# A fifth unit takes half of its gated features by eleven half products, in a new order of all steps

## The chip, the cores and the metric

The kernel runs on one core of one Trainium2 chip. The metric is the device time of one execution in microseconds (us), as the median over runs; lower is better. All arithmetic is fp32.

## The reference

Two blocks follow each other. The first is delta-rule attention over batch 4, 8 heads, 768 positions, head size 48; the second is a multiplicative feed-forward on the 3072 x 384 tokens that the first puts out.

```python
k_n = k / (norm(k) + 1e-06)
for t in range(S):                               # S = 768
    y[:, :, t] = q[:, :, t] @ state
    v_old = k_n[:, :, t] @ state
    state += beta_t * outer(k_n[:, :, t], v[:, :, t] - v_old)
x = y as (3072, 384)
a = x @ w1                                       # 384 -> 1024
b = x @ w2                                       # 384 -> 1024
out = ((a * b) @ w3) @ w_out                     # 1024 -> 1024 -> 384
```

## The kernel before

The engines are named as in the profile: PE multiplies matrices, DVE and POOL do elementwise work, ACT copies, SP starts transfers. The 768 positions go in 12 chunks of 64, for all 32 pairs of batch and head at once. Two chunks make a unit: 512 tokens. Units are numbered u = 0 to 5, and `last` is 5.

Each chunk m passes through the attention: its scores (`s`, lines 451 and 457), U and PT from them on DVE (463, 474), a triangular inverse per pair of chunks (`V`, the function `inverse`: 31 steps of two DVE instructions, lines 524 and 529, on a layout that goes out to DRAM and comes back, `Ud`, `Ub`), the corner blocks (`e`, 602 and 619), the chain that carries the state (`c`, line 672; 706, 717 and 738 on DVE) and the outputs (`y`, 777), which end as x transposed in `xT`.

Each unit then passes through the feed-forward. `w3 @ w_out` is folded into one matrix `w34` at the start (913), where all weights come in as fp64 and are converted piece by piece (`P0` to `P35`, 838 to 853). Units 0 to 4 compute a and b directly with `ab(u, jc)`: for a block of 128 features, three matmuls on `w1s` (934), a copy by ACT (946), three on `w2s`, and a multiplication on DVE (950). Unit 5 uses `features(u, p)`: for a pair p of blocks it splits tokens in two halves of 256 and forms a and b together by eleven half products of 128x256 (1074) where direct products would need twelve; sums of weights (`W`, `features_sums`, 1026 to 1037, on POOL) and of tokens (`X5`, `token_sums`, 1052, on POOL) feed it, DVE adds the pieces (1083), ACT copies them (1088 to 1110), and DVE multiplies (1118, 1131). Then `o(u)` computes the output by seven half products (1166), with sums of the a*b slabs (`S`, `slab_sums`, 1007: on POOL for units 0 to 4, on DVE for unit 5), and `result(u)` combines and stores (`x`, 1197 and 1182).

Products of the feed-forward go to four banks called `f` in turn (`ps_f`), the attention's to two double banks called `w` (`ps_w`). `in_turn` hands out buffers in a ring and skips those in `held`.

The order of all work is written out by hand. The string `ORDER` has one word for each step; each word names a part (`a42`: unit 4's `ab`, block 2; `V5`: the inverse of unit 5), and each time the word comes up, the part, a generator, goes on to its next `yield`:

```python
    for name in ORDER.split():
        step(name)
    in_text_order()
```

`in_text_order` ties the instructions of each engine together in that order, so the string sets the order on every engine.

Of the kernel before, what the change touches and what calls it, by code (L numbers as in the profile page):

```python
# [39 lines left out]
k0 g0 g0 g0 K0 V0 g0 k1 P12 K0 K0 beta K1 P0 g0 g0 K1 K1 g0 q1 P12 g0 P12 P12 beta g0 g0 beta N0  # L40
P8 P9 P8 P8 P8 P3 P0 P3 P3 P9 P0 s1 s1 s1 P9 s0 P3 P0 P13 P13 P13 s0 s0 V0 V0 V0 P1 P1 Q1 P1 P9
Q1 P10 P13 V0 V0 Q1 P1 P10 P2 P2 t0 t0 P2 P4 P4 V0 t1 P2 t1 V0 P4 P4 h1 t4 t4 N0 P6 f0 P7 P10
P10 P5 t2 t5 P18 V0 V0 P11 P6 V0 P6 P6 N0 P16 P19 V0 P7 P7 P5 P5 P5 q0 V0 t5 h1 P18 f2 P11 V0
P18 P7 t2 V0 f0 P14 h1 P22 P18 P19 f0 V0 P11 V0 V0 P11 P19 V0 V0 V0 P16 P16 P17 f2 f2 t10 t10
P23 Q0 Q0 t3 P19 t11 V0 P16 Q0 V0 t3 P22 P22 P22 P14 V0 V0 V0 f1 V0 V0 P23 P21 t8 P15 f1 P14 t11
P17 P17 f5 f5 V0 V0 f1 V0 V0 P17 t8 P15 V0 h0 V0 V0 P14 f5 P26 t6 P23 P20 V0 q2 P27 k2 t6 t9 t14
t9 v0 V0 P23 f4 f4 t14 f4 t15 t15 P21 P15 P15 t7 q3 V0 v1 Q2 Q2 V0 e0 h0 h0 e0 Q2 g1 e0 g1 t7 g1
f3 e0 e0 K2 P27 K2 e1 e0 e0 n0 e1 k3 f7 P27 n0 e1 c0 e1 P21 e1 f7 V1 g1 c0 y0 P28 c0 P20 P25 f7
P20 P20 P29 f3 P33 y0 n1 n1 P21 g1 c0 c1 y0 g1 g1 K2 f3 P28 P28 P28 P34 c1 t13 t13 t12 t12 P25
P27 K3 K3 K3 e1 s2 g1 P25 P29 P35 g1 P25 P33 f6 f6 P29 P29 e1 g1 N1 Q3 Q3 c1 y0 s2 s2 s2 P34 c1  # L50
s2 s2 f6 Q3 s3 K2 P30 P34 P34 P26 P26 P24 y1 y1 s3 P30 P31 N1 P33 N1 s3 b6 b6 P33 P35 P35 u2 P35
s3 s3 s3 Q0 P30 P30 c1 b4 b4 P24 P24 u3 P24 y1 b5 b5 b5 V1 P26 y1 V1 b5 P31 V1 P32 b6 b6 P31 b4
b0 b0 c1 b3 b4 b3 b7 V1 V1 b7 V1 V1 a02 V1 a02 V1 a03 V1 a05 V1 k4 V1 a00 V1 V1 P32 P32 a03 V1
b1 a00 a05 V1 V1 V1 V1 a04 V1 b1 c2 P32 P31 a04 a04 a04 a01 a01 T T T v2 n2 a02 T V1 k5 a07 a07
V1 v3 a02 V1 V1 a03 a03 V1 V1 V1 V1 V1 V1 a06 a06 b2 V1 b2 a07 a07 V1 a01 V1 V1 V1 a01 p4 p4 b2
n3 V1 V1 b2 a00 a00 a05 a05 g2 g2 g2 g2 a06 n2 b1 b1 b0 e2 b0 a06 g2 b3 b3 b7 b7 o0 g2 c2 n3 x0
e2 e2 g2 g2 o0 d4 e2 g2 e2 g2 o0 S0 S0 S0 e2 c2 d4 S0 S0 e3 S0 S0 x0 S0 S0 S0 S0 e3 e3 S0 S0 d4
p5 c2 c2 e3 c2 x0 S0 o0 c3 S0 e3 c3 o0 e3 N2 y2 c3 x0 o0 d4 p5 y2 S0 c3 y3 x0 x0 x0 d5 d5 s4 s4
o0 x0 y3 s4 s4 d5 d5 s4 s4 N2 s5 y3 u4 s5 V2 s5 s5 s5 N2 s5 c3 u5 V2 x0 p6 x0 a14 p6 a14 a14 a14
a13 a13 V2 V2 V2 V2 V2 a12 a12 V2 a16 a16 V2 V2 V2 V2 V2 V2 V2 a15 V2 a15 a11 a11 V2 V2 V2 V2 V2  # L60
V2 V2 V2 V2 v5 x0 V2 a10 V2 V2 k6 V2 v4 V2 V2 V2 V2 a17 a17 a15 a15 a10 k7 d6 d6 d6 a10 a10 c3
S1 n5 n4 a13 a12 a12 a13 V2 e4 a17 e4 a11 g3 g3 g3 g3 a11 Q3 c4 g3 g3 n4 c4 e4 a16 a16 e5 e4 e4
e4 o1 x1 S1 a17 S1 S1 S1 e5 e5 S1 e5 d6 n5 g3 c4 c4 g3 o1 S1 c4 V3 c4 g3 e5 e5 o1 p7 g3 N3 c5 p7
# [28 lines left out]
def kernel(  # L92
# [48 lines left out]
    turns, held = {}, set()  # L141

# [354 lines left out]
    def inverse(j):  # L497
# [15 lines left out]
        if j < 2:  # L513

            V = two_banks().rearrange("p a (s t) -> p (a s) t", t=BS)
            held.add(("w", turns["w"]))
# [14 lines left out]
        if j == 0:  # L531
            for x in range(4):
                dve.transpose(
                    out=TTpair[quarter(x), :, :, :, quarter(x % 2)].rearrange(
                        "s m r h t -> s t m (r h)"
                    ),
                    in_=V[quarter(x)].rearrange("p s t -> p t s"),
                )
                if x == 3:
                    held.clear()  # L540
                yield
            return
        if j < 2:
# [3 lines left out]
            held.clear()  # L547
# [417 lines left out]
    def weight_sums():  # L965
# [14 lines left out]
        Ts["T3"] = kperm[:].rearrange("p b a x d -> p (b a x d)")  # L980
# [12 lines left out]
    def slab_sums(u):  # L993
        for out_, x, y, op in (
# [4 lines left out]
        ):  # L999
            for i in range(HF if u < LU else HF // 2):  # L1000
                if u < LU:
                    o_, x_, y_ = (
# [356 lines left out]
```

## Time and profile before

| | before |
|---|---|
| median of 3 runs | 558.1 us (556.59 to 558.62) |
| profiled execution | 557.83 us, span 556.1 us |
| busy: PE, DVE, POOL, ACT | 533.6, 343.7, 169.7, 145.7 us |
| granted clock of PE | 1.00 |

The profile shows one execution. Busy times are shares of the span from the first to the last instruction; the execution's own time is 1.7 us longer than that span. Line numbers are those of the kernel before unless a passage speaks of the changed one, where most lines lie 7 to 30 further down (934 is 941, 950 is 957, 1074 is 1104, 1083 is 1113, 1166 is 1196, 1197 is 1227).

### The profile page before, as it was taken

What the parts mean: (1) busy time and instruction counts of PE and PEld (TensorE: products, weight loads), DVE (VectorE), ACT (ScalarE), POOL (GpSimd) and SP (SyncE); (2) the same over time, 40 slices, a digit from 0 to 9 for tenths busy, and PEclk for the clock granted to TensorE, in tenths of its full rate; (3) what the DMA queues carried; (4) which work ended last, traced back from release to release, by engine and by line L of the source; (5) the groups of instructions that cost most, each with busy time, mean ns of one, the idle gap of its engine ahead of it and who ended that gap; (6) DMA issues with size and microseconds to landing.
All of it is one profiled execution on the core that took longest, in us unless ns stands there. A gap on an engine that the chain in (4) does not pass through costs nothing.

```text
span 556.1 us, 19932 instructions
## 1 busy us (share of the span) xinstructions
PE 533.6 (96%) x8732; PEld 390.8 (70%) x8732; DVE 343.7 (62%) x800; ACT 145.7 (26%) x291; POOL 169.7 (31%) x213
## 2 busy tenths in 40 slices
PE   6699999999999999999999999999999999989997
PEld 5556667788998544888444897445995447988897
DVE  6799738589546498574995354885373973213552
ACT  2786567531121120220111211202201102212200
POOL 7574443527730002812102522004540027420000
PEclk9999999999999999999999999999999999999999
DMA  9999956594423593453745453605307222020001
GB/s 189 339 307 230 158 140 150 128 160 55 96 48 55 119 147 72 67 88 89 122 74 100 70 91 80 126 38 83 51 15 154 26 60 38 18 58 1 0 2 57
DMA packets 191527, 54.22 MB, mean 98 GB/s; under 512 B 178928, under 2 KB 185072, under 8 KB 191440
## 3 DMA queue, kind: packets, MB, share of 16 engines
q1 hardware_dynamic: 189328, 52.56, 46.3%
q8 instruction: 68, 1.11, 0.9%
q10 hardware_dynamic: 2112, 0.39, 0.5%
q14 instruction: 19, 0.16, 0.1%
HBM read 41.78 MB, written 9.96 MB: 93 GB/s over the span
## 4 chain that ended last, share of the span: by engine, by line
PE 93%; DVE 3%; issue 2%; DMA 2%; ACT 0%; SPq 0%; DVEq 0%
PE ps_f L934 38%; PE ps_f L1166 20%; PE ps_f L913 7%; PE ps_w L672 6%; PE ps_w L777 4%; PE ps_f L1074 4%; PE ps_w L619 3%; PE ps_w L1074 2%; PE ps_w L451 2%; PE ps_f L369 1%; PE ps_w L457 1%; PE ps_f L904 1%; DMA beta_fm<-in_beta_dram 1%; PE ps_w L409 1%; PE ps_w L1166 1%
## 5 line engine op out<-in xcount | busy, mean ns | idle before, releaser
L934 PE MATMUL ps_f<-xT,w2s 128*128 128x512 f32 (+1 forms) x288 | 106.9, 524 | 0.0
L934 PE MATMUL ps_f<-xT,w1s 128*128 128x512 f32 (+1 forms) x288 | 106.7, 524 | 0.0
L934 PEld LDWEIGHTS ps_f<-xT,w2s 128*128 128x128 f32 x288 | 54.1, 190 | 46.5 <-issue 41.6
L934 PEld LDWEIGHTS ps_f<-xT,w1s 128*128 128x128 f32 x288 | 54.0, 190 | 45.3 <-issue 41.6
L1007 POOL TENSOR_TENSOR ab<-ab 128x256 f32<-128x256 f32 x80 | 56.4, 731 | 78.7 <-DVE ab L950 73.8
L946 ACT COPY ab<-ps_f 128x512 f32<-128x512 f32 (+1 forms) x48 | 24.3, 515 | 134.4 <-PE ps_f L934 130.3
L1166 PE MATMUL ps_f<-w,ab 128*128 128x192 f32 x320 | 57.3, 332 | 1.9 <-DVE osb L1197 1.3
L1166 PEld LDWEIGHTS ps_f<-w,ab 128*128 128x128 f32 x320 | 51.6, 190 | 3.3 <-issue 2.4
L524 DVE TENSOR_TENSOR tb<-Vb,Ub 128x31 f32<-128x31 f32 (+15 forms) x124 | 43.0, 347 | 15.4 <-DMA Ub<-Ud 11.5
L529 DVE TENSOR_TENSOR Vb<-Vb,tb 128x31 f32<-128x31 f32 (+15 forms) x124 | 43.0, 346 | 4.3
L913 PE MATMUL ps_f<-wo,w3T 128*128 128x384 f32 x128 | 43.5, 491 | 0.4 <-ACT w3T L907 0.4
L1166 PE MATMUL ps_f<-room,ab 128*128 128x192 f32 x240 | 42.8, 332 | 0.0
L950 DVE TENSOR_TENSOR ab<-ab,ps_f 128x512 f32<-128x512 f32 (+1 forms) x48 | 27.4, 589 | 24.0 <-PE ps_f L934 24.0
L1166 PEld LDWEIGHTS ps_f<-room,ab 128*128 128x128 f32 x240 | 38.7, 190 | 0.7
L913 PEld LDWEIGHTS ps_f<-wo,w3T 128*128 128x128 f32 x128 | 23.5, 190 | 15.4 <-ACT w3T L907 0.5
L301 POOL TENSOR_TENSOR sq<-ktok 128x384 f32<-128x384 f32 x24 | 19.7, 835 | 43.5 <-DMA out_dram<-osb 16.9
L658 POOL TENSOR_TENSOR vtok<-vtok,n 128x384 f32<-128x384 f32 x24 | 19.8, 832 | 39.5 <-DMA vtok<-in_v_dram 39.5
L635 ACT COPY T<-ps_w 32x512 f32<-32x512 f32 x24 | 13.8, 577 | 67.2 <-PE ps_w L619 46.2
L795 ACT COPY xT<-ps_w 112x256 f32<-112x256 f32 x48 | 14.3, 384 | 65.0 <-PE ps_w L777 61.7
L451 PE MATMUL ps_w<-KQ 48*64 48x128 f32 x320 | 21.9, 274 | 1.8 <-DVE PT L474 1.5
L717 DVE TENSOR_TENSOR X<-ps_w,wt 128x768 f32<-128x768 f32 x12 | 11.5, 956 | 19.4 <-PE ps_w L672 12.9
L1197 DVE TENSOR_TENSOR room<-room,ps_f 128x384 f32<-128x384 f32 (+1 forms) x13 | 7.0, 537 | 26.4 <-PE ps_f L1166 26.4
(170 smaller groups left out, 805.9 us busy)
## 6 DMA issues: line engine op xcount, KB each, us to landing
vtok<-in_v_dram SPq DMA_DIRECT2D x24, 192.0 KB, 4.4
out_dram<-osb SPq DMA_DIRECT2D x23, 192.0 KB, 2.6
ktok<-in_k_dram SPq DMA_DIRECT2D x44, 96.0 KB, 3.4
raw<-in_moe_w_dram SPq DMA_DIRECT2D x8, 512.0 KB, 6.2
raw<-in_moe_w_dram SPq DMA_DIRECT2D x18, 192.0 KB, 4.5
raw<-in_moe_w_out_dram SPq DMA_DIRECT2D x7, 384.0 KB, 5.3
Ud<-U SPq DMA_DIRECT2D x40, 64.0 KB, 2.8
Ub<-Ud SPq DMA_DIRECT2D x5, 512.0 KB, 4.2
```

The costliest lines, as they stand in the source:

```text
L451: pe.matmul(ps[half(z), 0, n : n + 128], lhsT=x[:, 0, :], rhs=x.rearrange("p j t -> p (j t)"), start=True, stop=True,)
L524: dve.tensor_tensor(out=tv, in0=V[:, 0 : s + 1, s : s + 1].to_broadcast([P, s + 1, n]), in1=U[:, s, s + 1 : BS].unsqueeze(1).to_broadcast( ...
L529: dve.tensor_tensor(out=o, in0=o, in1=tv, op=ALU.subtract)
L672: pe.matmul(out(ps, r, h, z), lhsT=lhs(r, h, z), rhs=rhs(r, h, z), start=True, stop=True,)
L777: i = pe.matmul(region(h, z, r), lhsT=lhs, rhs=rhs, start=part[n] not in part[:n], stop=part[n] not in part[n + 1 :],)
L913: pe.matmul(ps[:, 0:DM], lhsT=w3Ts[jc, kc // 4][:, kc % 4 * P : kc % 4 * P + P], rhs=wo(kc), start=(kc == 0), stop=(kc == KF - 1),)
L934: pe.matmul(ps[:].rearrange("p b c t -> p b (c t)"), lhsT=w[:, m, js], rhs=x[:, m, :, c0:c1].rearrange("p b c t -> p b (c t)"), start=(m = ...
L946: act.copy(out=t, in_=ps)
L950: dve.tensor_tensor(out=t, in0=t, in1=ps, op=ALU.mult)
L1007: (dve if u == last else pool).tensor_tensor(out=o_, in0=x_, in1=y_, op=op)
L1074: pe.matmul(ps[:, j, :], lhsT=w[j], rhs=x, start=first and j == 0, stop=j == 1, skip_group_check=not first,)
L1166: pe.matmul(ps[b][:, b, :], lhsT=ab_of(u, HF * f + i, t0), rhs=ws_[w][:, i], start=first and i == 0 and (b == 0 or n == "F"), stop=i == HF ...
```

## The change

Four things change. `LU`, the first unit that uses half products, goes from 5 to 4: unit 4 takes blocks 0, 1, 4 and 5 directly (`a40` to `a43`) and the pairs p = 1 and p = 3 by `features` (`a44`, `a45`). The multiplications of pair 1 of unit 4 run on POOL, those of pair 3 on DVE. Unit 4's slab sums are eight of 128x256 on POOL and four of 128x512 on DVE. The rooms for sums of tokens move from one `KQ` buffer to one `ktok` and one `X` buffer, and that for the sum T3 of the weights from `kperm` to a `PT` buffer; these are taken out of their rings by `hold`. The differences in the first block of `w2s` become a part of its own (`Z`), a pair of blocks at a time. And `ORDER` is new from end to end.

```diff
...
-k0 g0 g0 g0 K0 V0 g0 k1 P12 K0 K0 beta K1 P0 g0 g0 K1 K1 g0 q1 P12 g0 P12 P12 beta g0 g0 beta N0
...
+k0 K0 k1 K1 K0 g0 P12 K0 beta beta g0 g0 g0 g0 g0 g0 g0 K1 K1 g0 P12 P12 g0 beta N0 P8 P0 P0 q1
...
+    def hold(tag):
+        held.add((tag, turns[tag]))
+
+    def release(tag):
+        held.difference_update([x for x in held if x[0] == tag])
...
-        Ts["T3"] = kperm[:].rearrange("p b a x d -> p (b a x d)")
...
+        def one(i, j, by):
+            out_, x, y, op = sums[j]
+            o_, x_, y_ = (abs_[u, HF // 2 * f + i, z] for z, f in (out_, x, y))
+            by.tensor_tensor(out=o_, in0=x_, in1=y_, op=op)
+
+        if u == last:
+            for k in range(4 * (HF // 2)):
+                one(k % (HF // 2), k // (HF // 2), dve)
                 yield
-
-    LU = last
+            return
+        for j in range(4):
+            out_, x, y, op = sums[j]
+            for i in range(HF // 2 if u >= LU else HF):
+                o_, x_, y_ = (abs_[u, HF * f + i][:, tokens(z)] for z, f in (out_, x, y))
+                pool.tensor_tensor(out=o_, in0=x_, in1=y_, op=op)
+                yield
+            if u >= LU:
+                one(1, j, dve)
+                yield
+
+    LU = 4
     shared = []
 
     def room_of_tokens():
         if not shared:
-            x = in_turn(work, [P, B, NP, 2, C], "KQ", 3, "tsum")
-            x = x[:].rearrange("p b a j t -> p (b a j t)")
-            shared.extend((x[:, 0:CW], x[:, CW : 2 * CW], x[:, 2 * CW : 2 * CW + C * B]))
+            for tag, n, name in (("ktok", 4, "tmp"), ("X", 2, "first")):
+                x = in_turn(work, [P, NR, H, D], tag, n, name)
+                hold(tag)
+                shared.append(x[:].rearrange("p r h d -> p (r h d)"))
+            x = shared[0]
+            shared[0], shared[1] = x[:, 0:CW], shared[1][:, 0:CW]
+            shared.append(x[:, CW : CW + C * B])
         return shared
 
     def features_sums():
+        x = in_turn(work, [P, NR, H, C], "PT", 3, "T3")
+        hold("PT")
+        Ts["T3"] = x[:].rearrange("p r h t -> p (r h t)")
...
+
+    def first_block_differences():
+        for p in (1, 3, 0, 2):
+            c = slice(2 * P * p, 2 * P * p + 2 * P)
+            B11, B12 = w1s[:, 0, c], w2s[:, 0, c]
             pool.tensor_tensor(out=B12, in0=B12, in1=B11, op=ALU.subtract)
             yield
...
+        by = dve if u == last or p == KF // 2 - 1 else pool
...
-        (dve if u == last else pool).tensor_tensor(out=Y0, in0=Y0, in1=both(first), op=ALU.mult)
+        by.tensor_tensor(out=Y0, in0=Y0, in1=both(first), op=ALU.mult)
...
+            elif j < last and jc < 4:
+                parts[f"a{j}{jc}"] = lambda u=j, jc=jc + jc // 2 * 2: ab(u, jc, 0, 2)
+            elif j < last and jc < 6:
+                parts[f"a{j}{jc}"] = lambda u=j, p=2 * jc - 7: features(u, p)
...
```

What stands in a row on PE in unit 4, from o3's last product on (934 are the direct products, 672 the chain, 619 the corners). Before:

```order
L1166 MATMUL ps_f<-w_117,ab 128x192 x8
L934 MATMUL ps_f<-xT,w1s 128x512 x18
L672 MATMUL ps_w<-X,ktok 48x48 x32
L934 MATMUL ps_f<-xT,w1s 128x512 x3
L934 MATMUL ps_f<-xT,w2s 128x512 x3
L934 MATMUL ps_f<-xT,w1s 128x512 x3
L934 MATMUL ps_f<-xT,w2s 128x512 x18
L672 MATMUL ps_w<-S,KQ 64x48 x32
L619 MATMUL ps_w<-T_108,U 33x32 x32
```

In the changed kernel, from the last but one of o3's products on (941 are the direct products, 1104 the half products, 1196 those of `o`, 679 the chain):

```order
L1196 MATMUL ps_f<-room,ab 128x192 x8
L941 MATMUL ps_f<-xT,w1s 128x512 x3
L1196 MATMUL ps_f<-w_117,ab 128x192 x8
L679 MATMUL ps_w<-X,ktok 48x48 x32
L293 MATMUL ps_f<-wt,ident 64x16 x2
L941 MATMUL ps_f<-xT,w1s 128x512 x9
L941 MATMUL ps_f<-xT,w2s 128x512 x12
L679 MATMUL ps_w<-S,KQ 64x48 x32
L1104 MATMUL ps_f<-xT,w1s 128x256 x2
L1104 MATMUL ps_f<-xT,w2s 128x256 x2
L1104 MATMUL ps_f<-xT,room 128x256 x2
L1104 MATMUL ps_f<-xT,w1s 128x256 x4
```

Two of o3's products now stand behind chunk 11's scores instead of one; 24 direct matmuls remain of 48, all ahead of the second group of the chain, and the half products follow it.

On DVE the steps of V5 (524 and 529, in the changed kernel 531 and 536) and the multiplications of unit 4 between them. Before, around the 20th and 21st steps:

```order
L524 TENSOR_TENSOR tb<-Vb,Ub 128x240
L529 TENSOR_TENSOR Vb<-Vb,tb 128x20x12
L950 TENSOR_TENSOR ab<-ab,ps_f 128x512
L524 TENSOR_TENSOR tb<-Vb,Ub 128x231
L529 TENSOR_TENSOR Vb<-Vb,tb 128x21x11
```

In the changed kernel, around the 21st step:

```order
L531 TENSOR_TENSOR tb<-Vb,Ub 128x231
L536 TENSOR_TENSOR Vb<-Vb,tb 128x21x11
L957 TENSOR_TENSOR ab<-ab,ps_f 128x512 x4
L531 TENSOR_TENSOR tb<-Vb,Ub 128x220
L536 TENSOR_TENSOR Vb<-Vb,tb 128x22x10
```

And in the changed kernel, at V5's end (1113 are the adds of `features`, 609 the transposes for the corners):

```order
L531 TENSOR_TENSOR tb<-Vb,Ub 128x31
L536 TENSOR_TENSOR Vb<-Vb,tb 128x31
L1113 TENSOR_TENSOR first<-first,ps_f 128x512
L1113 TENSOR_TENSOR y_6048<-y_6048,ps_f 128x512
L1113 TENSOR_TENSOR tmp<-tmp,ps_f 128x512
L1113 TENSOR_TENSOR y_6066<-y_6066,ps_f 128x512
L609 STREAM_TRANSPOSE T_108<-TT_89 128x512
```

One multiplication stood inside V5 and seven behind it; now four stand inside it, and the first pair's four adds right behind it, ahead of the corners' transpose.

On SP at the start the loads of keys, beta, queries and pieces of weights (838, in the changed kernel 845). Before:

```order
L838 DMA raw<-in_moe_w_dram 128x1024
L1251 DMA beta_fm<-in_beta_dram 16x12x64 x2
L838 DMA raw<-in_moe_w_out_dram 128x768
L1233 DMA X<-in_q_dram 32x8x96 x4
L838 DMA raw<-in_moe_w_dram 128x1024
L838 DMA qperm<-in_moe_w_dram 128x1024
L838 DMA raw<-in_moe_w_out_dram 128x768
```

In the changed kernel:

```order
L845 DMA raw<-in_moe_w_dram 128x1024
L1281 DMA beta_fm<-in_beta_dram 16x12x64 x2
L845 DMA raw<-in_moe_w_dram 128x1024
L845 DMA raw<-in_moe_w_out_dram 128x768
L1263 DMA X<-in_q_dram 32x8x96 x4
L845 DMA raw<-in_moe_w_out_dram 128x768
L845 DMA spare<-in_moe_w_out_dram 128x768
```

A second piece of w3 now stands ahead of the queries, and two pieces of w_out follow them.

More of the change, by code (lines that the diff above doesn't have):

```diff
@@ L515, in inverse @@
             V = two_banks().rearrange("p a (s t) -> p (a s) t", t=BS)
-            held.add(("w", turns["w"]))
+            hold("w")
             for i in range(0, BS, BS // 2):
@@ L539, in inverse @@
                 if x == 3:
[L540 removed]
+                    release("w")
                 yield
@@ L993, in slab_sums @@
     def slab_sums(u):
-        for out_, x, y, op in (
+        sums = (
             ((1, 0), (1, 0), (1, 1), ALU.add),
@@ L998, in slab_sums @@
             ((0, 1), (0, 1), (0, 0), ALU.subtract),
[L999 to L1002, printed above, removed]
[L1003 to L1010 removed]
+        )
+        def one(i, j, by):
[5 more added lines that the diff above has]
+                one(k % (HF // 2), k // (HF // 2), dve)
+                yield
+            return
[9 more added lines that the diff above has]
+    LU = 4
     shared = []
@@ L1130, in features @@
         yield
-        (dve if u == last else pool).tensor_tensor(out=Y1, in0=Y1, in1=both(tmp), op=ALU.mult)
+        by.tensor_tensor(out=Y1, in0=Y1, in1=both(tmp), op=ALU.mult)
         abs_[u, p, 0], abs_[u, p, 1] = Y0, Y1
```

108 lines of the change are left out of this document (52 added, 56 removed).

## The prediction

> **What bounds the kernel now.** I read the page's totals first, then the chain that ended last, then the busy time of each engine by stage (columns: window, its length, busy time and count of PE, PEld, DVE, ACT, POOL, granted clock, DMA share, GB/s), then what PE waited for (total, times, longest).
>
> ```profile
> PE 533.6 (96%) x8732; PEld 390.8 (70%) x8732; DVE 343.7 (62%) x800; ACT 145.7 (26%) x291; POOL 169.7 (31%) x213
> PE 93%; DVE 3%; issue 2%; DMA 2%; ACT 0%; SPq 0%; DVEq 0%
> 0.00:25.00 25.00, 14.30 (x468) 12.28 (x469) 17.01 (x41) 11.58 (x21) 15.88 (x27) 1.00 0.93 253
> 420.00:460.00 40.00, 40.00 (x157) 17.89 (x155) 27.41 (x72) 4.49 (x8) 4.10 (x5) 1.00 0.39 76
> 460.00:496.00 36.00, 34.37 (x955) 30.44 (x955) 9.13 (x15) 8.01 (x18) 15.44 (x22) 1.00 0.14 30
> PE ps_w L409 <- issue: 5.4, 2, 4.4
> PE ps_f L369 <- DMA ktok<-in_k_dram: 4.3, 2, 4.1
> PE ps_w L451 <- DVE PT L474: 1.5, 4, 0.5
> PE ps_f L1166 <- DVE osb L1197: 1.3, 1, 1.3
> ```
>
> PE is busy for 533.6 of 556.1 us and is 93% of the chain. In unit 4's stretch (420 to 460 us) it has no idle time at all, at clock 1.00, while DVE uses 27.41 of 40 us and POOL 4.10. So work taken off PE there is time, unless PE then meets a wait; and DVE is the engine with the least room. Outside the start PE's waits are small: 1.5, 1.3 and less. The first 25 us hold 10.7 us of idle PE, beside DMA that is busy for 0.93 of the time.
>
> **The algebra.** The chain gives unit 4's own products (start, us, what), and a window filtered to the half products of unit 5 gives the price of the new form.
>
> ```profile
> 417.62 2.80 PE ps_f L1166 x16
> 420.42 15.45 PE ps_f L934 x36
> 435.87 0.87 PE ps_w L672 x64
> 436.73 23.37 PE ps_f L934 x54
> 460.11 1.08 PE ps_w L672 x64
> 461.87 2.77 PE ps_f L934 x6
> 420.00:496.30 76.30, 0.17 (x1) 0.34 (x2) 1.00 0.27 55
> 496.30:534.30 38.00, 38.00 (x176) 32.99 (x175) 1.00 0.03 10
> ```
>
> Removed: half of unit 4's 96 passes (each product of 128x512 is two passes on PE). All of them take 15.45 + 23.37 + 2.77 = 41.59 us, 0.433 each; half is 20.80. Added: two pairs of blocks by eleven half products, 44 passes a pair. Unit 5 does four such pairs in 176 passes, back to back in 38.00 us of a 38.00 us window that begins and ends about where they do; with the 0.17 that the neighbouring window holds of the same line, 38.17. A pair is 9.54, a half product (four passes) 0.867, two pairs 19.09. On PE this is 19.09 - 20.80 = -1.71 us. As PE is the chain there, -1.71 is the gain before waits.
>
> **DVE in unit 4.** These are the prices of one instruction (busy, mean ns) by operation and shape:
>
> ```profile
> L950 DVE TENSOR_TENSOR ab<-ab,ps_f 128x512 f32<-128x512 f32 x32 | 21.0, 675 | 17.8 <-PE ps_f L934 17.8
> L1083 DVE TENSOR_TENSOR y<-y,ps_f 128x512 f32<-128x512 f32 x4 | 2.8, 688 | 7.6 <-PE ps_f L1074 7.6
> L1131 DVE TENSOR_TENSOR y<-y,tsum 128x512 f32<-128x512 f32 x4 | 2.8, 692 | 0.1
> L1088 ACT COPY tsum<-ps_f 128x512 f32<-128x512 f32 x4 | 2.3, 586 | 16.5 <-PE ps_f L1074 11.2 <-DVE y L1118 5.3
> L1026 POOL TENSOR_TENSOR kperm<-w2s 128x512 f32<-128x512 f32 x2 | 2.5, 1270 | 11.8 <-DVE KQ L355 11.8
> L1007 POOL TENSOR_TENSOR ab<-ab 128x256 f32<-128x256 f32 x80 | 56.4, 731 | 78.7 <-DVE ab L950 73.8 <-PE ps_f L1166 4.9
> ```
>
> Four of eight multiplications (0.675) go; eight adds (0.688), two multiplications of the second pair (0.692) and four slab sums (0.69) come: about -2.7 + 9.7 = +7.0 us on DVE. It had 12.6 free in 420 to 460 and 26.9 in 460 to 496, so the sum fits; what counts is the order. DVE works in order, and V5, the triangular inverse of 31 steps, now has the four remaining multiplications inside it and the first pair's adds behind it. How V5 lies today (DVE rows: start, us, line, operation; then the SP row that starts its transfer):
>
> ```profile
> 428.42 0.19 DVE L524 TENSOR_TENSOR tb<-Vb,Ub 128x31 f32<-128x31 f32 x1 [6.81 <-DMA Ub<-Ud]
> 444.03 0.68 DVE L950 TENSOR_TENSOR ab<-ab,ps_f 128x512 f32<-128x512 f32 x1
> 444.63 0.39 DVE L524 TENSOR_TENSOR tb<-Vb,Ub 128x231 f32<-128x231 f32 x1
> 445.49 0.39 DVE L524 TENSOR_TENSOR tb<-Vb,Ub 128x220 f32<-128x220 f32 x1
> 452.00 0.21 DVE L529 TENSOR_TENSOR Vb<-Vb,tb 128x31 f32<-128x31 f32 x1
> 452.12 1.28 DVE L950 TENSOR_TENSOR ab<-ab,ps_f 128x512 f32<-128x512 f32 x2
> 417.69 5.41 SPq L491 DMA_DIRECT2D Ud<-U  x8
> 424.67 0.34 SPq L510 DMA_DIRECT2D Ub<-Ud  x1
> ```
>
> I roll both engines forward from the end of chunk 11's scores, which is where the 2.80 us row of the chain begins (417.62). V5 starts 428.42 - 417.62 = 10.8 after it; in the new order one store of a result, which stood ahead of the eight stores of U on SP, stands between them and the load of Ub; it is hidden, since SP is through with them at 423.10 and the load starts at 424.67. So I keep the 10.8. Its first 21 steps take 445.49 - 428.42 less the 0.60 by which the multiplication pushed them (444.03 to 444.63): 16.5, to 27.3. The four multiplications end at 28.0, 28.6, 29.3 and 29.9 (0.64 apart by the 1.28 for two). PE meanwhile does two products of o3 (2 x 2.80), 48 passes (20.8), and two groups of the chain (0.87 + 1.08): 28.35 us. Its first half product wants the bank that the first multiplication frees at 28.0: no wait, with 0.36 to spare; the next banks have more.
>
> V5's last ten steps take 452.21 - 445.49 = 6.7, to 36.6. Only then come the four adds of the first pair, ending at 37.2, 37.9, 38.5 and 39.2. PE ends that pair at 28.35 + 9.54 = 37.9, and the second pair's first product takes the bank that the third add frees at 38.5: a wait of 0.6. POOL's multiplication (1.27, by its 128x512 row) runs from 37.9 to 39.2; the copy behind it (0.59) ends at 39.9, and PE, which needs it before its third half product, arrives at 38.5 + 2 x 0.867 = 40.2. That fits. POOL's second one waits for the fourth add and for a scaling of v (128x384, at most 0.95 by the POOL rows of that shape below): to 41.4, its copy 42.0, wanted at 43.7. So this stretch costs **+0.6**; the bounds are 0, if V5 comes as much earlier, and +4, if V5 starts some 3.4 later, since a late V5 is paid one for one.
>
> **What else moves.** POOL loses eight slab sums and gains four token sums (128x256, so 0.73 each by its row), two multiplications and smaller pieces of the weight differences, in a stretch with 36 us free: 0. The new buffers for the token sums take one of the four key buffers and one of the two X buffers; a load then waits for an older reader; SP has no share in the chain, so 0, and at worst a wait like that for keys, 4.1, in place of one load's cover. o4's last product still waits for its DVE reader (the 1.3 row stays). The waits of the scores for DVE move about as the pieces around them do: 0, bounds -1.5 (all of that row) and +1.5. The new order of the start moves the loads of weights on SP past one another and so PE's steps; there I have only these two pieces of the chain:
>
> ```profile
> 13.95 0.95 issue
> 16.96 4.42 issue
> q8 instruction: 68, 1.11, 0.9%
> ```
>
> Both precede matmuls of line 409, in the stretch where DMA is busy for 0.93 of the time. The 68 packets of the instruction queue are 16 KB each (1.11 MB / 68), one for about 256 instructions. I take 0 for the start, bounds -3.5 (the long one becomes as short as its sister, 4.42 - 0.95) and +3.5 (the short one becomes long). [...]
>
> **Sum.** Against the profiled execution's 557.83 us (its span is 556.1; the median of the runs shown is 558.1, 0.3 higher): 557.83 - 1.71 + 0.6 = **556.7 us**. A difference under 0.5%, 2.8 us, can hardly be told from none, so up to 555.3 is faster and from 560.9 slower.
>
> **Rivals.**
> *V5's convoy (slower).* Anything that makes V5's first step late, the landing of its input Ub above all, makes the four multiplications late, and PE has no bank until they are done. Before, one multiplication stood inside V5, now four. It decides from 4.2 us late on (556.7 + 4.2 = 560.9). For it: DVE already waited 6.81 for Ub here, and the update of the state and a reader of o3's last product now stand ahead of V5 on DVE. Against: those pieces are through before 10.8 by the roll, and the load's 3.75 us (424.67 to 428.42) has no new transfer beside it. If V5 is 5 us late, 561.7; chance 0.14. Small waits of a wholly new order that I have not seen add 0.08 on that side.
> *The start (faster).* If the 4.42 wait shrinks to 0.95: 556.7 - 3.5 = 553.2. For it: the waits lie where loads crowd, and it is these loads that are reordered. Against: no row says what they wait for. Chance 0.28.
> *POOL beside V5.* In an earlier unit:
>
> ```profile
> 269.88 0.40 DVE L524 TENSOR_TENSOR tb<-Vb,Ub 128x231 f32<-128x231 f32 x1
> 270.31 0.90 DVE L529 TENSOR_TENSOR Vb<-Vb,tb 128x231 f32<-128x231 f32 x1
> 270.01 0.95 POOL L301 TENSOR_TENSOR sq<-ktok 128x384 f32<-128x384 f32 x1 [16.94 <-DMA out_dram<-osb]
> 274.40 0.42 DVE L529 TENSOR_TENSOR Vb<-Vb,tb 128x255 f32<-128x255 f32 x1
> 274.86 1.09 DVE L524 TENSOR_TENSOR tb<-Vb,Ub 128x256 f32<-128x256 f32 x1
> 274.84 0.83 POOL L301 TENSOR_TENSOR sq<-ktok 128x384 f32<-128x384 f32 x1 [3.88 <-DVE Vb L529]
> ```
>
> A step of V beside a POOL instruction takes 0.90 or 1.09 where its neighbour takes 0.40 or 0.42: +0.5 and +0.67. The token sums of unit 4 stand among V5's steps, where POOL had next to nothing. Three of them among its steps ahead of the adds cost up to 3 x 0.67 = 2.0, paid on PE: 558.7. Beside a multiplication, which reads one operand from PSUM, I expect no cost. Chance 0.10, inside "same". [...]
> *The saving is not there.* If a half pass cost as much as makes a pair 10.4, the gain is gone: 558.4. The 176 passes in 38.00 us, 0.217 against 0.433, speak against it; the 0.40 of the forecast includes this.
>
> **How the numbers follow.** Forecast 0.40 and POOL 0.10 end within 0.5%: same 0.50. Faster 0.28 (the start), slower 0.22 (V5, others). The range reaches from the start's 553.2, less 0.7 for scores that wait less, nearly to V5's 561.7: 552.5 to 561.5 leaves out about a tenth on each side. The likeliest cases alone lie between 555.3 and 559.
>
> **What would show it.** Line 1104 (the half products) should have 264 passes, the first 88 in about 19.1 us; PE should wait about 0.6 at the second pair for DVE's adds, and hardly at the first; V5's first step should come about 10.8 us behind chunk 11's scores; the multiplications inside it 0.6 apart. Wrong would be: a wait over 1 us of line 1104 for DVE (V5), steps of V5 near 0.9 beside line 1080 (POOL), or a changed "issue" at the start, which would swamp the rest.

## The result, and the profile after

The changed kernel takes 572.8 us in the median (570.95 to 574.22) where the kernel before takes 557.35 in the same session: 1.0273 times as long, 95% interval 1.0249 to 1.0298. The medians are 15.5 us apart. The forecast was 556.7. The profiled execution took 573.49 us with a span of 571.8, 15.7 more than before.

The page's totals, the chain's shares and two windows of the changed kernel, read as those of before, and then the second window of the kernel before:

```profile
PE 535.7 (94%) x8772; PEld 398.6 (70%) x8772; DVE 356.6 (62%) x810; ACT 148.0 (26%) x295; POOL 170.8 (30%) x213
PE 80%; DVE 8%; DMA 4%; issue 4%; ACT 1%; SPq 1%; POOL 0%; ACTq 0%; DVEq 0%; POOLq 0%
0.00:25.00 25.00, 12.36 (x465) 10.72 (x466) 17.87 (x42) 10.57 (x18) 13.65 (x26) 0.76 0.93 255
25.00:45.00 20.00, 15.63 (x116) 10.12 (x117) 16.02 (x43) 12.95 (x27) 12.27 (x11) 0.87 0.73 250
```

```profile
25.00:45.00 20.00, 19.11 (x202) 12.73 (x201) 18.87 (x56) 17.93 (x36) 12.60 (x11) 1.00 0.93 321
```

PE still has the most work, but its share of the chain fell from 93% to 80%. The first 45 us now have 17 us of idle PE, where they had 11.6. What PE waited for in the changed kernel (total, times, longest; the waits for keys at the start, 4.6 for 4.3, and some small rows are left out):

```profile
PE ps_w L416 <- issue: 7.2, 2, 4.1
PE ps_f L1196 <- issue: 3.7, 3, 1.6
PE ps_f L920 <- POOL wo L860: 3.3, 1, 3.3
PE ps_f L1196 <- DVE osb L1227: 1.8, 2, 1.3
PE ps_w L784 <- issue: 1.2, 1, 1.2
PE ps_w L679 <- issue: 1.1, 2, 0.8
PE ps_f L911 <- POOL w L860: 1.1, 1, 1.1
PE ps_f L1104 <- DVE ab L957: 0.9, 2, 0.8
PE ps_f L941 <- DVE wt L299: 0.7, 1, 0.7
PE ps_w L626 <- issue: 0.6, 1, 0.6
PE ps_w L458 <- issue: 0.5, 1, 0.5
```

And in the kernel before, its waits put down to issue beyond those of line 409 and its wait for POOL:

```profile
PE ps_w L672 <- issue: 0.8, 2, 0.5
PE ps_w L777 <- issue: 0.5, 1, 0.5
PE ps_w L451 <- issue: 0.3, 1, 0.3
PE ps_f L904 <- POOL w L853: 0.5, 1, 0.5
```

Adding up all rows of this view, in both traces, places the whole difference (the 5.5 us that each span has beyond its sum are alike):

| us of PE | before | changed | more |
|---|---|---|---|
| waits put down to issue | 7.0 | 14.3 | +7.3 |
| waits for POOL | 0.5 | 4.4 | +3.9 |
| waits for DVE | 4.0 | 6.0 | +2.0 |
| waits for DMA and ACT | 5.5 | 5.9 | +0.4 |
| busy | 533.6 | 535.7 | +2.1 |
| sum | 550.6 | 566.3 | +15.7 |

The largest row is one that an order of steps seems not to touch. Beyond the start these waits grew from 1.6 to 7.1 us. I therefore looked at each of them there, and numbered PE's instructions (passes, weight loads and semaphore instructions) from the trace. Gaps between the starts of two passes of over 0.45 us, counted from start to start and so a little longer than PE's idle time, that end 1.2 to 1.7 us behind a packet of the instruction queue:

```
before                                     changed
at us   gap   number   number mod 256      at us   gap   number   number mod 256
 97.4   0.75    3776      192               83.6   0.49    2497      193
102.0   0.60    4032      192              101.3   0.72    3521      193
168.1   0.67    6081      193              105.4   1.41    3777      193
251.3   0.55    9153      193              183.7   1.84    6592      192
474.1   0.50   16064      192              241.4   0.79    7873      193
                                           246.1   1.03    8129      193
                                           254.4   1.59    8640      192
                                           416.9   1.16   14017      193
sum 3.1                                    sum 9.0
```

All of them stand at the same place in a block of 256 instructions, and the gaps end 1.2 to 1.7 us behind a packet of 16 KB (1.13 MB in 69 packets on the changed kernel's page, 1.11 in 68 before). This looks as if PE had run out of instructions. So "theory F" below: a stretch of short matmuls uses up its instructions faster than they come, and the order decides how dense such stretches are. "Theory A" is that the loss comes from several places of the new order and not from unit 4's form; its rival B is that unit 4 and V5 cost it.

### The profile page after: what moved, and what is told of

Its sections match the earlier page's. It is cut to its first block, busy times and chain, and to the rows that moved or that the text cites. A ratio compares the mean times of both kernels' runs of the same rounds, so it can differ in the third digit from the quotient of the medians.

```text
span 571.8 us, 20047 instructions
## 1 busy us (share of the span) xinstructions
PE 535.7 (94%) x8772; PEld 398.6 (70%) x8772; DVE 356.6 (62%) x810; ACT 148.0 (26%) x295; POOL 170.8 (30%) x213
## 3 DMA queue, kind: packets, MB, share of 16 engines
q8 instruction: 69, 1.13, 0.9%
## 4 chain that ended last, share of the span: by engine, by line
PE 80%; DVE 8%; DMA 4%; issue 4%; ACT 1%; SPq 1%; POOL 0%; ACTq 0%; DVEq 0%; POOLq 0%
PE ps_f L941 29%; PE ps_f L1196 17%; PE ps_f L920 7%; PE ps_f L1104 6%; PE ps_w L679 5%; PE ps_w L784 4%; PE ps_w L626 3%; DVE tb L531 2%; PE ps_w L1104 2%; DVE Vb L536 2%; DMA Ub<-Ud 2%; PE ps_w L458 1%; PE ps_f L376 1%; DMA Ud<-U 1%; PE ps_w L464 1%
## 5 line engine op out<-in xcount | busy, mean ns | idle before, releaser
L941 PE MATMUL ps_f<-xT,w1s 128*128 128x512 f32 (+1 forms) x264 | 96.6, 518 | 0.4 <-DVE osb L1227 0.3
L941 PE MATMUL ps_f<-xT,w2s 128*128 128x512 f32 (+1 forms) x264 | 96.2, 517 | 0.7 <-DVE wt L299 0.7
L1020 POOL TENSOR_TENSOR ab<-ab 128x256 f32<-128x256 f32 x72 | 51.0, 733 | 140.9 <-DVE ab L957 116.0
L941 PEld LDWEIGHTS ps_f<-xT,w2s 128*128 128x128 f32 x264 | 49.7, 190 | 41.9 <-issue 37.1
L941 PEld LDWEIGHTS ps_f<-xT,w1s 128*128 128x128 f32 x264 | 49.4, 190 | 40.5 <-issue 35.9
L1196 PE MATMUL ps_f<-w,ab 128*128 128x192 f32 x288 | 53.0, 332 | 5.6 <-issue 3.7
L1196 PEld LDWEIGHTS ps_f<-w,ab 128*128 128x128 f32 x288 | 46.7, 190 | 7.7 <-issue 6.9
L531 DVE TENSOR_TENSOR tb<-Vb,Ub 128x31 f32<-128x31 f32 (+15 forms) x124 | 43.8, 353 | 12.1 <-DMA Ub<-Ud 8.2
L920 PE MATMUL ps_f<-wo,w3T 128*128 128x384 f32 x128 | 45.9, 509 | 3.7 <-POOL wo L860 3.3
L1196 PE MATMUL ps_f<-room,ab 128*128 128x192 f32 x216 | 39.5, 333 | 0.0
L920 PEld LDWEIGHTS ps_f<-wo,w3T 128*128 128x128 f32 x128 | 24.1, 196 | 19.7 <-POOL wo L860 3.5
L1196 PEld LDWEIGHTS ps_f<-room,ab 128*128 128x128 f32 x216 | 34.8, 190 | 0.8
L802 ACT COPY xT<-ps_w 112x256 f32<-112x256 f32 x48 | 14.3, 384 | 75.1 <-PE ps_w L784 75.1
L665 POOL TENSOR_TENSOR vtok<-vtok,n 128x384 f32<-128x384 f32 x24 | 20.0, 837 | 33.4 <-DMA vtok<-in_v_dram 33.4
L531 DVE TENSOR_TENSOR tb<-ps_w,Ub 128x31 f32<-128x31 f32 (+15 forms) x62 | 21.0, 339 | 4.4 <-ACT ps_w L525 3.0
```

The source lines that it names most:

```text
L531: dve.tensor_tensor(out=tv, in0=V[:, 0 : s + 1, s : s + 1].to_broadcast([P, s + 1, n]), in1=U[:, s, s + 1 : BS].unsqueeze(1).to_broadcast( ...
L665: pool.tensor_tensor(out=nv[:, r], in0=nv[:, r], in1=scale_of(ns, c)[:, r].unsqueeze(2).to_broadcast([P, H, D]), op=ALU.mult,)
L920: pe.matmul(ps[:, 0:DM], lhsT=w3Ts[jc, kc // 4][:, kc % 4 * P : kc % 4 * P + P], rhs=wo(kc), start=(kc == 0), stop=(kc == KF - 1),)
L941: pe.matmul(ps[:].rearrange("p b c t -> p b (c t)"), lhsT=w[:, m, js], rhs=x[:, m, :, c0:c1].rearrange("p b c t -> p b (c t)"), start=(m = ...
L1020: pool.tensor_tensor(out=o_, in0=x_, in1=y_, op=op)
L1196: pe.matmul(ps[b][:, b, :], lhsT=ab_of(u, HF * f + i, t0), rhs=ws_[w][:, i], start=first and i == 0 and (b == 0 or n == "F"), stop=i == HF ...
```

## The experiments

### Which stretch of the order costs it

The order is a list of words, so two orders can be joined: the first n words of one, then the other without those words. Unit 4's form does not change by that.

```diff
-ORDER: the new 1410 words
+ORDER: old words 1 to n, then the new words that are left    (n = 70, 120, 580, 1000, 1030, 1070, 1117)
```

120 words: 

> The changed kernel with the first 120 of its order's 1410 words replaced by those of the kernel before (about the first 40 us: loads, first keys, first folds); the rest in the new order. Theory A (the 15.5 us come from several places of the new order: about 7.5 us before 50 us, where PE waits longer for pieces of its instruction stream and for a converted weight and its granted clock falls to 0.5; about 3 us each in 50 to 200 and 200 to 300 us, most of it waits called issue; 1 in 300 to 415, 3 in unit 4; less 2.0 of saved work): 565 us, granted clock 1.00. Theory B (unit 4's new form and V5 cost it all): 572, as the changed kernel.

580 words: 

> The changed kernel with the first 580 words from the kernel before (to the end of unit 0, about 182 us). Theory A: start and the stretch to 182 us are as before, so 572.8 - 7.5 - 3 = 562 us, and the issue waits at 101, 105 and 184 us are gone or as small as before (0.5 to 0.7). Theory B: 572.

1070 words: 

> The changed kernel with the first 1070 words from the kernel before (all up to chunk 10's scores): only unit 4 in the new form and all behind it in the new order. Theory A: 557.4 - 2.0 of work + 2.7 of waits for DVE and issue = 558 us, between 556 and 560. Theory B: 571 to 573.

And the other way round, in the old kernel: 

> The kernel before with the first 583 words of the new order (to the end of unit 0), unit 4 as it was. Theory A: 557.4 + 7.5 + 3 = 568 us, with the granted clock of PE near 0.5 in 15 to 25 us. Theory B: 557.

A second session narrowed the start and looked for unit 4 alone: 

> The changed kernel once more, beside the others of this call, as their reference: 571 to 574 us. Its issue waits past 60 us should end 1.3 to 1.5 us behind a fetch and stand at instruction numbers 192 mod 256 again, in much the same places.

> The changed kernel with only the first 70 words from the kernel before (about the first 23 us: loads, first keys and scores). Theory S1 (the start is lost in the first 23 us, by the longer issue wait at 13 us, 3.1 for 0.95, and the halved clock): nearly all of the 5.6 us that 120 words gave back, 567 to 568. Theory S2 (it is lost at 28 to 39 us, where PE waits 1.1 and 3.3 us for pieces of w3 and w_out that DVE and POOL convert behind other steps): 571 to 573, with those two waits still there.

> The changed kernel with the first 1000 words from the kernel before (up to the end of V4, about 355 us). Theory A (unit 4's new form saves about 2 us where the order brings no new wait): 557 to 560, depending on the wait for a block of instructions near 406 us, which was 1.2 in the changed kernel and 2.0 with 580 words. Rival B (the form costs as such): 560 to 563.

> The same with 1030 words (to about 365 us, all direct products of unit 3 in the old order). Theory A: 556 to 559; rival B: 560 to 563.

Measured, each ratio against the kernel before in the same session:

| kernel | median us | ratio to before, interval |
|---|---|---|
| changed, again | 575.2 | 1.0279 (1.0250 to 1.0308) |
| 70 old words (to 23 us) | 567.9 | 1.0162 (1.0147 to 1.0177) |
| 120 old words (to 40 us) | 567.2 | 1.0162 (1.0139 to 1.0185) |
| 580 old words (to 182 us) | 561.8 | 1.0058 (1.0035 to 1.0081) |
| 1070 old words | 560.5 | 1.0044 (1.0023 to 1.0066) |
| 1000 old words | 558.7 | 1.0007 (0.9989 to 1.0025) |
| 1030 old words | 559.3 | 1.0013 (0.9984 to 1.0043) |
| kernel before, 583 new words | 567.8 | 1.0171 (1.0144 to 1.0197) |

Theory B falls: with 1000 old words, unit 4's new form and all behind it cost nothing that can be measured, and the kernel before loses 9.8 us by the new order of its first 182 us alone. On the way from the changed kernel to 1000 old words about 6 us come back with the first 70 words, none with the next 50, about 6 with those to 580, and about 3 with those to 1000. In the second trace of the changed kernel the gaps stand at 192 again (8.8 us beyond 60 us), five of seven within 2 us of their places above.

Half of the difference between the 120-word and the 580-word kernel is as theory F says. PE's waits put down to issue with 120 old words, and then with 580:

```profile
PE ps_w L416 <- issue: 6.2, 2, 4.1
PE ps_f L1196 <- issue: 3.6, 4, 1.2
PE ps_w L784 <- issue: 1.7, 2, 1.5
PE ps_w L626 <- issue: 0.6, 1, 0.6
PE ps_w L464 <- issue: 0.5, 1, 0.5
PE ps_w L679 <- issue: 0.3, 1, 0.3
```

```profile
PE ps_w L416 <- issue: 5.3, 2, 4.1
PE ps_f L1196 <- issue: 4.2, 3, 1.7
```

The rows of L784, L626, L464 and L679 are gone. The two profiled executions, 565.9 and 558.6 us in span, are 7.3 us apart (the medians 5.4). The waits put down to issue fall by 3.4 of them, from 12.9 to 9.5, and those for DVE by 3.8, from 8.4 to 4.6; theory F does not speak of the second part, and no run looked into it. Beyond 60 us the gaps at block ends add up to 9.1 us with 120 words and 5.2 with 580. Of these 5.2, the two at 327 and 406 us (1.52 and 2.02) go with 1000 words, where 3.5 are left.

Repeating one stretch alone did not add up as neatly. Old words for 121 to 580 only, and a move of single words in the start:

> The changed kernel with words 121 to 580 in the order of the kernel before (about 40 to 182 us), start and end in the new order. Theory A: the 5.4 us of that stretch go as they did between the cuts at 120 and 580 words: ratio to before 1.017 to 1.019, and issue waits of 50 to 200 us as before, about 3.6 us. Rival (what the stretch loses depends on the start): 1.022 or more.

```diff
-P18 h1 V0 V0 V0 V0 P10 V0 V0 P7 P1 P9 P6 P5 P4 t1 P11 P10 f0 f2 P5 t5 V0 t1 V0 P6 P7 P4 t2
+P18 h1 P10 P7 P1 P9 P6 P5 P4 t1 P11 P10 f0 f2 P5 t5 t1 P6 P7 P4 V0 V0 V0 V0 V0 V0 V0 V0 t2
```

> The changed kernel with eight words of V0 moved behind the conversion of the last four pieces of w_out (they stood ahead of it on DVE, whose first V0 step waited 3.0 us for ACT); PE's order is unchanged. Theory S2: PE's wait of 3.3 us for POOL's converted w_out, at 36 to 39 us, falls to about 1, V0's later end is covered: 2 to 3.5 us less than the changed kernel, ratio to before 1.022 to 1.024. Rival (what the start loses lies ahead of 25 us): no change, 1.028.

The first gave 571.7 us, 1.0236 (1.0201 to 1.0271): some 2 us came back, which the intervals hardly tell from none, of the 5 to 6 that the same stretch is worth behind the old start. The second gave 576.3 us, 1.0329 (1.0299 to 1.0359), no faster than the changed kernel (1.0279, 1.0250 to 1.0308). The two largest of PE's waits there:

```profile
PE ps_w L416 <- issue: 6.3, 2, 4.1
PE ps_f L911 <- POOL w L860: 5.0, 3, 2.9
```

The wait for w_out (`wo`) is gone, and waits for pieces of w3 (`w`) of 5.0 us have taken its place. The granted clock of that run was also 0.5 from 44.8 to 51.6 and from 106.2 to 113.0 us, and PE was busy for 540.2 us, 4.5 more than in the changed kernel. So a conversion that no longer comes late for PE let another one come late. With the 70 old words the profiled execution is 6.4 us shorter than that of the changed kernel: waits for POOL fall from 4.4 to 0.8, waits put down to issue from 14.3 to 12.4, PE's busy time from 535.7 to 534.1. So more than half of what the start loses are conversions that come late for PE, POOL's step being the last of each. Which words of the 70 do it was not found.

### Is it the clock

The granted clock is 0.5 from 13.1 to 26.7 us of the changed kernel, and the views of the kernel before print 1.00 there. That is no difference between the two. The trace of the kernel before holds no record of the clock ahead of 25.07 us, and the same passes take the same time in both, slower ahead of 25 us than behind it. Rows of the windows up to 25 us and behind it, before and then changed:

```profile
L369 PE MATMUL ps_f<-ident,X 64*48 64x64 f32 x64 | 2.0, 313 | 0.0
L369 PE MATMUL ps_f<-ident,X 64*48 64x64 f32 x64 | 1.1, 218 | 0.0
```

```profile
L376 PE MATMUL ps_f<-ident,X 64*48 64x64 f32 x64 | 2.0, 313 | 0.0
L376 PE MATMUL ps_f<-ident,X 64*48 64x64 f32 x64 | 1.1, 218 | 0.0
```

So the kernel before is as slow ahead of 25 us, and a printed 1.00 can be a record that is missing. The kernel with 120 old words, where I expected 1.00, and that with 1000 show the 0.5 too; the latter in its window of 15 to 20 us:

```profile
15.00:20.00 5.00, 1.88 (x128) 1.64 (x120) 2.62 (x9) 3.77 (x8) 1.88 (x2) 0.50 1.03 402
```

It ends at 1.0007 all the same. The executions of the kernel before beside these runs agree: of 58, 29 have a mean clock of 0.980 to 0.988 and 28 one of 0.997 to 1.000, and these take 558.4 and 558.3 us in the mean.

A second drop does cost. In the changed kernel PE stands still for 3.3 us amid the folds (the row of L920 above), the clock is 0.5 from 40.4 to 43.8 us, and the folds run slower. The same group before and after:

```profile
L913 PE MATMUL ps_f<-wo,w3T 128*128 128x384 f32 x128 | 43.5, 491 | 0.4 <-ACT w3T L907 0.4
L920 PE MATMUL ps_f<-wo,w3T 128*128 128x384 f32 x128 | 45.9, 509 | 3.7 <-POOL wo L860 3.3 <-ACT w3T L914 0.3
```

That is 2.4 us more, of which half of the 3.4 us at 0.5 explains 1.7 (an estimate); PE's whole busy time grew by 2.1, since other parts of it fell. This stretch of half clock lasts 3.41 us, others inside the kernels 6.83 (44.8 to 51.6 us of the run with V0 moved) or 13.65 (from 13.1 us in the changed kernel). PE was busy for 1.0 of the 3.41 us ahead of this drop. The changed kernel with idle matmuls (below) dropped at 104.6 us, beside waits of 0.73 and 0.83: two passes of 128x512 took 1.91 us there and 1.05 at 184, four score passes 0.42 and, from 108 us on, 0.28. So a long wait is not what it takes.

### How fast instructions come

Short matmuls were put behind the kernel's own last product, first all of one kind into one place:

```diff
+    for i in range(512):
+        ...
+        pe.matmul(ps[0:D, 0:C], lhsT=w1s[0:D, 0, 0:D], rhs=w1s[0:D, 1, 0:C], start=True, stop=True)
```

> The kernel before with 512 more matmuls of 48x64 at its end (2048 PE instructions, since each fp32 matmul is two loads and two passes; their results are not used). PE's own pace for such passes is 16 to 17 ns (64 in 1.08 us): 17 us. Theory F (PE's instructions arrive in blocks of 256, one in about 4.2 us at best, and PE waits for them): 8 blocks, 28 to 34 us behind the kernel's own last product, in steps with issue waits at instruction numbers 256 apart, each ending 1.3 to 1.5 us behind a fetch of 16 KB; total about 583 us. Rival (the issue waits have nothing to do with the supply of instructions): 17 us in one piece, total about 571.

> As the kernel with 512 short matmuls at its end, and two matmuls of 128x512 ahead of every 32 of them (32 in all, 27.7 us of PE work by the rows of the direct products). Theory F: the long ones fill the time in which the next block comes: 17.3 + 27.7 = 45 us behind the kernel's own last product and hardly an issue wait, so only 11 to 17 us more than the short ones alone. Rival: 27.7 more than the short ones alone, whatever those take.

They took 104.7 and, with long ones between them, 61.0 us for 1024 passes, and 660.7 and 653.1 us in all, without a wait. PE itself needs 13.1 us for a block of the first (104.7 / 8) and 10.6 for one of the second (5.6 us for 68 passes, with the long ones among them), so this pair tells nothing on theory F. By the prediction's 0.433 us for a pass of 512 columns, 64 columns take 54 ns (an estimate), and 102 at the granted clock of 0.53 that the first run had; measured are 59.6 and 102. So these passes keep the usual pace for their columns, and it is the kernel's own short passes that come faster. Those go to changing places, but no run shows that this is the reason. The next three repeat a real group of scores, whose products go to different places:

```diff
+    for i in range(24):
+        for _ in range(LONG):                       # 0, or 2 in the mixed run
+            pe.matmul(pl[:], lhsT=w1s[:, 0, 0:P], rhs=w1s[:, 1, 0:512], start=True, stop=True)
+        ps, r = two_banks(), i % 2
+        ...                                         # the 24 matmuls of scores(11), as they are
```

> The kernel before with the score products of its last chunk repeated 24 times behind its last product (24 matmuls each, into the two double banks in turn, results not used): 2304 PE instructions, 9 blocks of 256. [...] PE's own pace for one such group is about 0.9 us, 22 us in all. Theory F (a block of 256 instructions comes every 4.2 us at best): 32 to 38 us, with issue waits at instruction numbers 256 apart, each ending 1.3 to 1.5 us behind a fetch. Rival: 22 us, no issue wait.

> The same 24 groups with two matmuls of 128x512 (1.73 us) ahead of each. Theory F: 24 x (0.9 + 1.73) = 63 us and hardly an issue wait; so 41.5 us of work more than the short run costs only 25 to 31 more. Rival: also 63, but 41 more than the short run.

> The same 24 groups alone, while SP issues 64 loads of keys and queries as the kernel does for four chunks (results not used). Theory F with transfers in the way: a fetch of instructions stands behind those loads, so a block takes longer than in the run without loads: by 0.5 us or more each, 4 us or more in all. Theory F without that: the same length as the run without loads, within 1 us.

The groups of the added lines in the short run, then in the mixed run (busy, mean ns, idle before):

```profile
L1344 PE MATMUL ps_w<-KQ 48*64 48x64 f32 x768 | 24.3, 219 | 4.0 <-issue 4.0
L1338 PE MATMUL ps_w<-KQ 48*64 48x128 f32 x384 | 23.8, 276 | 2.3 <-issue 2.3
```

```profile
L1331 PE MATMUL ps_f<-w1s 128*128 128x512 f32 x96 | 47.5, 617 | 0.0
L1344 PE MATMUL ps_w<-KQ 48*64 48x64 f32 x768 | 27.6, 221 | 0.0
L1338 PE MATMUL ps_w<-KQ 48*64 48x128 f32 x384 | 26.2, 275 | 0.0
```

The short run takes 30.8 us for 9 blocks, with seven issue waits (6.3 us), each at a block's end. In the mixed run there is none among the added groups: theory F holds on where waits come, and its rival falls. The transfers of the instruction queue begin at 561.11, 564.74, 568.48, 572.28, 576.26 and 579.81 us in the short run, one in 3.74 us; PE alone goes through a block in 2.45. With loads beside it they begin at 561.98, 566.09, 569.78, 574.16, 578.28 and 582.50, one in 4.10, and the run takes 33.4 us. So with loads a block takes 0.36 us longer, less than the 0.5 expected. That is one execution of each, and the run with loads had a granted clock of 0.5 from 577.5 to 584.4 us, where PE itself took 3.8 and 4.2 us for a block: its length is not the loads' alone, but the three intervals ahead of that are 4.06 in the mean. The two lengths were misjudged: the supply is a little faster than the 4.2 us that I read from the trace, and PE took 72.1 us in the mixed run for the 63 expected; where these 9 us go was not looked into.

### Filling the waits

```diff
+            pe.matmul(ps[0:32, 0, :].rearrange("p (a b) -> p a b", a=4), lhsT=zero[:],
+                      rhs=ident[:].unsqueeze(1).to_broadcast([P, 4, P]), start=True, stop=True)
```

> The changed kernel with four idle matmuls of 128x512 (zero weights, 0.87 us of PE each, 3.5 in all) put just ahead of four of its longest issue waits, at 105, 184, 254 and 417 us (1.41, 1.84, 1.59 and 1.16 us). Theory F: PE does them while it would have waited; the waits become 0.5, 1.0, 0.7 and 0.3 and the time stays within 0.7 us of the changed kernel's, 572.8 (ratio to before 1.027 to 1.029). Rival (a wait is a pause of its own): 576.3, ratio 1.033 to 1.034.

> The kernel before with the same four idle matmuls at the same four steps, where it has no such waits (0.5 at most). Theory F and rival alike: 2.5 to 3.5 us longer than before, 560.5 to 561.5. It is the control to the changed kernel with the same matmuls.

The changed kernel with them took 579.2 us, ratio 1.034 (1.0278 to 1.0403): the interval holds both theories. The control took 562.9, 1.0074 (1.0045 to 1.0104), 4.5 us more, since each of the idle matmuls took 1.05 us and not 0.87. In the trace the gap at 184 us went from 1.84 to under 0.4, but that at 254 stayed at 1.6 behind the filling, one of 1.79 came at 335, and a stretch of half clock came at 104.6. This test is inconclusive.

### Unit 4 with everything else old

> The changed kernel with the first 1117 words from the kernel before: all up to unit 4's first product in the old order, and only unit 4's new form (a43 to a40, the two pairs) and what follows in the new one. The wait of 1.7 us for a reader of o3 that the cut at 1070 words brought is gone. Theory A: 0.3% less to 0.2% more than before, 556 to 559 us: the saving of 2 us of work is there and little else. Rival B (the new form of unit 4 costs as such): 560 or more, as with the cut at 1070 words.

It took 572.5 us, 1.0242 (1.0219 to 1.0265). Not for unit 4's products: the cut itself brings two long waits.

```profile
PE ps_w L458 <- DVE PT L481: 5.5, 4, 4.4
PE ps_f L941 <- DVE wt L299: 4.5, 1, 4.5
```

With 1070 words a wait of 1.7 for a reader of o3 did the same on a small scale. Only the cuts at 1000 and 1030 leave unit 4 clean, and neither is faster than the kernel before beyond its interval.

## Why the prediction was wrong

**Unit 4: the mechanism was right, but its waits use up the gain.** Line 1104 has 264 passes, as forecast. The two pairs take from 459.29 to 480.1 us, 20.8, of which 0.7 are a corner's products: 20.1 for the 19.1 forecast, with small waits in it. V5, its multiplications and PE's first half products in the changed kernel:

```profile
429.15 2.87 PE L1196 MATMUL ps_f<-room,ab 128*128 128x192 f32 x16
440.80 0.19 DVE L531 TENSOR_TENSOR tb<-Vb,Ub 128x31 f32<-128x31 f32 x1 [1.72 <-DMA Ub<-Ud]
455.87 1.67 POOL L1080 TENSOR_TENSOR xT<-xT 128x256 f32<-128x256 f32 x2 [24.01 <-PE ps_f L941]
456.14 0.81 DVE L536 TENSOR_TENSOR Vb<-Vb,tb 128x240 f32<-128x240 f32 x1
457.62 0.77 POOL L1080 TENSOR_TENSOR tmp<-xT 128x256 f32<-128x256 f32 x1
457.83 0.81 DVE L536 TENSOR_TENSOR Vb<-Vb,tb 128x231 f32<-128x231 f32 x1
458.56 2.47 DVE L957 TENSOR_TENSOR ab<-ab,ps_f 128x512 f32<-128x512 f32 x4
459.29 1.13 PE L1104 MATMUL ps_f<-xT,w1s 128*128 128x256 f32 x4 [0.78 <-DVE ab L957]
```

V5 begins 11.65 us behind chunk 11's scores (10.8 forecast). Its steps beside POOL's token sums take 0.81 where their like took 0.40: the rival "POOL beside V5" came true, at three steps. The multiplications pay nothing, as expected: those of 128x512 that lie beside a POOL instruction for over 0.2 us take 673 ns in the mean in the kernel before (nine) and 679 in the changed one (seven), the others 676 and 677. The slower steps make the multiplications late: PE waits 0.78 ahead of the first pair, and 0.16 within the 20.1; the forecast wait of 0.6 at the second pair was under 0.1. The wait for N5's `wt`, 0.7, I did not foresee. So instead of -1.7 + 0.6 the stretch comes to -1.7 + 1.0 + 0.8 + 0.7 = +0.8, and the cut at 1000 words measured 1.0007: nothing clear of noise either way, but the 1.1 us of gain (0.998) lie outside its interval.

**V5's convoy** was not it: V5 came 0.85 us later than rolled, not 4.2. **The start (faster)** went the other way: the long wait shrank only from 4.42 to 4.14, and its short sister grew from 0.95 to 3.11. That is 1.9 us more, inside the bound of 3.5 that I had put there; the 0 that the sum took for the start is shown by no run. **The saving is not there** did not come true: PE is busy for 531.7 us with 1000 old words and for 533.6 before, 1.9 less.

**The step that failed** is "What else moves". It set every other part of an order that is new from end to end at 0, with bounds of 3.5 for the start and 1.5 for the scores, because I had looked only for waits that the trace of before showed at the places I rolled. Measured, it is about 15 us: some 6 by the first 70 words, where I had bounded the issue waits and not the converted weights on POOL (+3.9) and the slower folds behind them (+2.4); and some 9 by the words for 40 to 355 us, where I had taken "issue" for a matter of the start. Waits put down to issue are the largest part of the second, though between the cuts at 120 and 580 words waits for DVE fell as much. The row of the instruction queue stood in the prediction, with about 256 instructions to a packet (8732 loads and 8732 passes for 68); I did not ask how long a packet takes against how long PE takes for 256 short instructions. Beyond the start alone PE stands idle at the ends of blocks for 7.1 us in the changed kernel, and for 1.6 in the one before.

What stays open: how far each stretch's loss depends on those ahead of it (the stretch of 40 to 182 us gave back 2 us behind the new start, 6 behind the old), which words of the first 70 make the conversions late, and why the waits for DVE differ by 3.8 us between the kernels with 120 and 580 old words.

## What to carry to other kernels

When a change rewrites an order, the part that it is about is the smaller risk: every stretch that was fitted before is fitted no more, and a term "everything else: 0" needs a price from the stretches with the least slack, not from those that one looks at. In a kernel of many small matmuls, compare PE's time for each run of 256 instructions with the time in which a block comes (2.45 us against 3.74 in the short run), and put long products between dense groups (with them the added groups had no issue wait); a wait put down to issue is read with the instruction queue beside it. Old and new orders can be joined at a word, which finds the costly stretch in a few runs, though each cut can bring a wait of its own. A clock that the profile prints is checked against the time of the same passes in another stretch.

## What the runs showed of the hardware

- PE's issue waits beyond the start stand at one place of every 256 of its instructions (192 or 193 mod 256) and end 1.2 to 1.7 us behind a 16 KB packet of the instruction queue. These packets began 3.74 us apart in a quiet stretch and 4.10 beside loads that kept the DMA engines busy for 0.62 of the time (one execution of each, the second with a granted clock of 0.5 in part of it). PE went through 256 short instructions in 2.45.
- 512 matmuls of 48x64 that all write one place of a bank take 59.6 ns a pass between long ones (61.0 us for 1024) and 102 alone, where the granted clock was 0.53. The scores' passes of 48x64 and 48x128, to changing places, took 20 to 21 with the waits taken off (30.8 - 6.3 us for 1152), less than the 54 that 64 columns come to by the 0.433 of a 512-column pass (an estimate).
- PE's granted clock fell to 0.5 for 3.41 us behind the wait of 3.3 us amid the folds, which took 2.4 us more than before. It fell as well beside waits of 0.73 and 0.83 us (104.6 us of the changed kernel with idle matmuls; four score passes took 0.42 us there and 0.28 behind it). Where the trace has no record of it, the views print 1.00: the passes of line 369 took 313 ns ahead of 25 us and 218 behind it, as in the changed kernel with its 0.5.
